# A longer hand-written order for the first phase (60 products and ten weight pieces), and the load of u moved ahead

## The chip, the cores and the metric

One core of a Trainium2 chip runs the whole kernel. The metric is the time of one execution in microseconds (us). The engines are named as in the profile: PE multiplies matrices and transposes, DVE, ACT and POOL work element by element, SP issues the transfers (DMA). Each engine works through its own queue of instructions in order, and waits at an instruction until what it needs has been signalled.

## The reference

```python
# attention: B=2, H=8, S=768, D=48, a state of D x D per head
cur = k_t (outer) v_t, weighted by u
y_t = r_t . (state + cur)
state = w_t * state + k_t (outer) v_t
# x: [1536, 384], the outputs of all heads side by side
# first network: w_in 384 x 2048, w_out 2048 x 384
x = max(0.01 * (x @ w_in), x @ w_in) @ w_out
# second network: a gate over 8 experts, normalised 8 times over rows and columns
P = exp(x @ w_gate - max); 8 times: P /= P.sum(1); P /= P.sum(0); P *= N / E
out = sum over e of P[:, e] * (max(x @ w1[e], 0) @ w2[e])   # 384 -> 1024 -> 384
```

## The kernel before

The program has three phases on PE. The first, here called the front, computes the attention in 12 blocks of 128 tokens (even blocks are one batch, odd ones the other) and starts the first network under it. The second, the middle, finishes the first network and the gate; its first gate product is L579. The third runs the eight experts.

The front's order is written by hand. `FRONT` is a table of single operations, split at the blanks, and the program issues them in that order; each goes to the queue of its engine. Three kinds of names stand in it.

- `7k` is an operation of attention block 7. PE: `w`, `k`, `r` turn the block's inputs (L369), `m` is the scores (L414), `B` turns the keys (L425), `y` the outputs (L446, L455), `z` the new state (L463), `x` turns the result (L496). DVE: `q` and `p` are the two running products of the decays (L387, L392), `K` and `R` weigh keys and r with them (L396), `c` sums r times u times k per head (L510), `A` and `D` mask the scores (L429), `Y` adds to the output (L472), `U` to the state (L487), `l` splits off the low half of the result (L299). POOL: `a`, `b` multiply r, k and u (L504, L505), `v` is L511. ACT has `W`, `S`, `s`, `t`, `C`, `h`. `9Lv` is a load of block 9's v by SP (L349).
- `c6f` is a step of the conversion of weight piece 6. The first network's weights arrive as 64-bit floats; each of 16 pieces (768 KB) is loaded into one of two staging buffers `stg` (L255, SP) and split into a high and a low part. DVE does `a` (L264), `b` (L267), `d` (L270) and `f` (L274), ACT `e`, `g`, `h`, POOL `m` (L278) and `l` (L280). The step `m` is the last reader of the staging buffer, so the load of piece n+2 waits for the `m` of piece n. Pieces come in fours: two of w_in, two of w_out.
- `u5.1P` is a product of the first network: group 5 of a list of column quarters and token groups, half 1. `P` is a first-layer product of 18 matmuls (L531), followed by `r` (ACT), `t` (DVE, L1083), `h` (ACT, L1085), `l` (POOL, L1087). `u5.2p` is a second-layer product of 12 matmuls (L546), followed by `q`, its sum (ACT for the first quarter, DVE L1094 otherwise). One `P` or `p` is one slot; slots go on in the middle.

PE's results in the front lie in six banks that are handed round in turn: an operation that needs a bank takes the one that came free longest ago, and so waits for the operation that frees it.

The middle is not ordered by hand. Its operations are issued slot by slot, `PIECE_AT` names the slot at which the conversion of each piece beyond the table is written, and the framework's scheduler sets the final order on each engine; it may put such an operation between operations of the table. `FRONT_SLOTS` is the number of slots and `FRONT_PIECES` the number of pieces that the table covers; the next two pieces' loads are issued right behind the table.

Of the kernel before, what the change touches and what calls it, by code (L numbers as in the profile page):

```python
# [67 lines left out]


FRONT = """  # L70
0w 0a 0k 0W 0r 0q 0b 1w 0s 0I 0K 0p 0B 0c 0C c0a 0t 0R 1r 1W c0b 0m 0v 1q c0g c0d 1a 1s 1k 0A 0z c0e 0D 1b 1I 1K
0y 0U c0f 1p c0m 1B 2Lw 1C 0Y 2Lk 1t 1z 1c 1R c0h 1v 2Lr c1a c0l 2Lv 0x 1U c1b 1m 0h c2L 2a 0l 2w c1g 1A 2k 2W
2r 1D 2b 2q 1y c1d 2s 2I 2K 3Lw c1e 1Y 2B 3Lk 2p 2S 1x 3Lr 2c 2C 3w 2R 3Lv 1h 2v 2t c1f 2m 3W 1l 3a 3k 3q 2z c1m
3r 2A u0.0P 3s 2D 2U 3b c1h c3L 3I 3K 2y u0.0r 3p c1l u0.0t 3t 3c u0.0h c2a 3B 3S 4Lw 2Y u0.0l u0.1P 3R 4Lk 3C
c2b 3v 4Lr c3a 2x c2g 4Lv 3m c2d u0.1r c3b 2h 4w c2e 4k 4a u0.1t 2l 4W 3z 3A u0.1h 4b 4r 3D c3g 4q 3y u0.1l 3U
4s 4I c2f 4K c2m 4S 5Lw 3Y 4B 4p 5Lk 3x 4C 5Lr c2h 4z 4c 5Lv 3h c2l 4R 4t c4L 3l 4m c3d 5w 4v 4A 5k c3e 5r 4D 5a
u2.0P 5W c3f 5b 5q 4y u2.0r c3m u2.0t 5s 4U 5I 5K c3h c5L u2.1P 5p 5S c3l 4Y 5t 5c 4x 5R 5B 5v 4h c4a u0.0p 5C
6Lw 4l 6Lk c4b 5m u0.0q 6Lr c5a c4g 5z c4d 6Lv 5A c4e 6w 5D 6k 6W u0.1p 5U 6a 6q 5y u0.1q 6b c4f 6s 6I 6K c4m 6r
6p 6S 7Lw 6B u0.2p 7Lk 6C c4h 5Y 7Lr 6z 6c u0.2q c4l u2.0h 6R 7Lv 5x 6t 6U 7w c6L 6m 5h c5b 7W u2.0l 7k 5l c5g
7r 6A u1.0P 6D 6v 7q 7a 6y c5d u1.0r 7b 7s u1.0t c5e 7I 7K 7p u1.0h 7B 7S 8Lw u1.0l u3.0P 6Y 8Lk 7c 7t 7R 7v 8Lr  # L80
u2.1r c5f 7C 6x 8Lv 7m 6h u2.1t c5m 6l 8w u2.1h 8k 7A 8W 7z 7D u2.1l c5h c7L 8q 8r 7y 8a 7U 8s 8I 8K c5l 8p
u2.0p 8S 9Lw 9Lk 8B u2.0q 8b u1.1P 7Y 8C 9Lr 8R 8t 8c 9Lv c7a 8v c6a 7x u1.1r 8m 9a 7h u1.1t 9w 7l u1.1h 9k 8A
9b 9W 8z 8D 9q 9r u1.1l 8y 8U 9s 9I 9K u3.0r 9p 9B 9S 10Lw u2.1p u3.0t 8Y 10Lk 9t 9c 8x 10Lr 9R 9C 9v u2.2p
u2.1q c7b 8h 10Lv 9m 8l c7g c7d 10a c6b u2.2q 10w c7e 10k 9z 10W 10b 9A c6g 10r 9D u3.1P 10q 9U 10s 10I 9y 10K
u3.1r 10p u3.1t 10t 10c u4.0P 10S 11Lw 9Y 10R 10v 11Lk c7f 11Lr 9x u4.0r c6d 10m c7m 9h 11Lv u4.0t c6e 9l 11w
11k 10A u4.0h u4.1P 11a 11W 10D c7h c6f u4.0l 11q 10y 11b 11s 11I 11K c7l 11p 11r 11S u5.0P c6m 10Y 11t 11c 10x
11R u5.1P 10h 11v c6h c8L 10l c6l 11m u5.1r u5.1t u6.0P 11A 11D 11y c8a c8b c8g c8d u1.0p 11Y c8e c8f 11x u1.1p
11h u1.0q c8m 11l u1.2p u1.1q c8h u6.1P u1.2q u3.0h c8l u3.1h u7.0P u3.0l u7.1P u3.1l u4.1r u4.1t u4.1h u5.0r
u3.0p u4.1l u5.0t u3.1p u3.0q u6.0r u6.0t u3.2p u3.1q u4.0p u5.0h u3.2q u5.1h u5.0l u4.1p u4.0q u5.1l u6.1r
u4.2p u4.1q u6.1t u7.0r u5.0p u4.2q u7.0t u6.0h u6.1h u6.0l u5.1p u5.0q u6.1l u7.1r u5.2p u5.1q u7.1t u8.0P  # L90
u5.2q u7.0h u7.1h u7.0l u6.0p u8.0r u7.1l u8.0t u6.1p u6.0q u6.2p u6.1q u7.0p u8.0h u6.2q u8.0l u7.1p u7.0q
u7.2p u7.1q u8.1P u7.2q u9.0P u8.1r u8.1t u8.1h u9.1P u8.1l u9.0r u9.0t u9.0h u8.0p u9.0l u9.1r u9.1t u8.1p
u9.1h u8.0q u9.1l u8.1q
""".split()

FRONT_SLOTS, FRONT_PIECES = 46, 9

GATES = {
    "0/P7": "cs_pe", "0/P14": "cols1", "-1/Q:0:0": "cols2", "0/P0": "rows1", "-1/Q:0:2": "rows2",
# [11 lines left out]
def tile_rwkv__leaky_moe__sinkhorn_moe(  # L111
# [41 lines left out]
    def src(x, i):  # L153
        return x[i % B, :, (i // B) * T : (i // B + 1) * T, :].rearrange("h t d -> t h d")
# [53 lines left out]
    def forward(general, ctx):  # L208
# [43 lines left out]
        def load_words(src):  # L252
            st = stage()
            sv = st.bitcast(I32).rearrange("p (a n t) -> p a n t", a=src.shape[1], t=2)
            nc.sync.dma_start(out=sv.rearrange("p a n t -> p a (n t)"), in_=src)  # L255
            return sv
# [89 lines left out]
        def load_tile(i, names):  # L346
            for n in names:
                t = A.nat[i % 2][n]
                nc.sync.dma_start(out=t[:, :, 0:D], in_=src({"w": w, "k": k, "r": r, "v": v}[n], i))  # L349
# [373 lines left out]
        def piece_load(n):  # L723
            kind, q, h = pieces[n]
            if kind == "i":
                c0 = 2 * (q * FQ + h * NW)
                pst[n] = load_words(w_in32[:, :, c0 : c0 + 2 * NW])
            else:
                pst[n] = load_words(w_out32[:, q * NJ + h * NR : q * NJ + (h + 1) * NR, :])
# [23 lines left out]
        if general:  # L753
            piece_load(0)
        else:
            load_tile(0, "wrk")
            load_tile(1, "w")
            piece_load(0)
            nc.sync.dma_start(
                out=ub.rearrange("p h d -> p (h d)"), in_=u.rearrange("h d -> (h d)").partition_broadcast(P)  # L760
            )
            load_tile(1, "r")
            load_tile(0, "v")
            load_tile(1, "vk")
# [48 lines left out]
        def attach(sl, pe, post, first=False):  # L813
            q = extra.setdefault(sl, [])
            if first:
                q.insert(sum(1 for x in q if x[2]), (pe, post, True))
            else:
                q.append((pe, post, False))

        PIECE_AT = (-7, -4, -1, 0, 0, 1, 1, 5, 44, 56, 57, 60, 81, 85, 85, 90)  # L820

        last = {q: max(n for n, s_ in enumerate(slots) if order[s_[1]][0] == q) for q in range(NQ)}
        lastp1 = {q: max(n for n, s_ in enumerate(slots) if order[s_[1]][0] == q and s_[0] == "p1") for q in range(NQ)}
        for n, (kind, q, h) in enumerate(pieces):
            at = PIECE_AT[n]
            assert at + 1 < need[(kind, q, h)]
# [52 lines left out]
        def w_load(s):  # L879

            st = stage()
            va = st[:, :PW].rearrange("p (c f) -> p c f", c=KD)
            vb = st[:, PW:].rearrange("p (i n) -> p i n", i=2)
            if s < NH:
                e, m = divmod(s, NJ2 // 2)
                nc.sync.dma_start(out=va, in_=w1[e].rearrange("(c p) f -> p c f", p=P)[:, :, m * 2 * P : (m + 1) * 2 * P])
            if s > 0:
                e, m = divmod(s - 1, NJ2 // 2)
                nc.sync.dma_start(
                    out=vb, in_=w2[e].rearrange("(j p) n -> p j n", p=P)[:, 2 * m : 2 * m + 2, :]  # L890
                )
            raw[s] = (va, vb)
# [98 lines left out]
        attach(close_slot, none, open_wb)  # L991
        s4 = PIECE_AT[-1] + 2
        attach(s4, none, lambda: w_load(0))
# [382 lines left out]
    with ExitStack() as es:  # L1376
        forward(False, es)
    flag = nc.values_load(oki)
    with tc.If(flag == 0):
        with ExitStack() as es:  # L1380
            recurrence(es)
        with ExitStack() as es:
            forward(True, es)
# [29 lines left out]
```

## Time and profile before

| | before |
|---|---|
| median of 3 runs (lowest to highest) | 1106.45 us (1106.14 to 1107.18) |
| the profiled execution | 1104.46 us |
| its span in the trace | 1102.7 us |
| PE busy in the span | 1066.0 us (97%) |
| DVE, ACT, POOL busy | 815.4, 485.9, 544.6 us |
| PE's mean granted clock | 0.981 of full |
| the gate's first product (L579) starts at | 308.95 us |

The span is 1.76 us shorter than the execution it was taken from. Some 794 us of the span, from the gate's first product on, hold the gate and the experts, and the change lies ahead of that. A busy PE may still run at half clock, so busy shares are read together with the granted clock.

### The profile page before, as it was taken

How to read it: one execution, taken by the hardware profiler on the slowest of the kernel's cores; microseconds unless marked ns; L12 is line 12 of the kernel's file. 1: busy time of each engine (PE TensorE's matmuls, PEld its weight loads, DVE VectorE, ACT ScalarE, POOL GpSimd, SP SyncE). 2: the span in 40 equal slices, each digit the busy share in tenths (PEclk: the TensorE clock that was granted, in tenths of full speed). 3: DMA queues.
4: the chain of work that ended last, by engine and by line, in shares of the span. 5: the costliest groups of instructions: out<-in, count | busy, mean ns of one | idle time of the engine just before them, and what ended most of it. 6: DMA issues, size and time to landing. Idle time of an engine off the chain costs nothing.

```text
span 1102.7 us, 16354 instructions
## 1 busy us (share of the span) xinstructions
PE 1066.0 (97%) x6295; PEld 980.7 (89%) x6295; DVE 815.4 (74%) x1352; ACT 485.9 (44%) x894; POOL 544.6 (49%) x632
## 2 busy tenths in 40 slices
PE   7899989999999899999999999999999999999997
PEld 6798989999997688899999999999999999999997
DVE  7989954275346998777776777767777777777776
ACT  4546544344334344454444444444444444445431
POOL 6548465258442445464445554455544555445500
PEclk8889989999999999999999999999999999999999
DMA  7446221012000000010000100001000010000002
GB/s 193 94 116 142 69 86 58 1 58 79 23 1 1 29 29 29 29 58 30 29 29 29 58 30 29 29 29 58 30 29 29 29 54 33 29 29 29 15 1 90
DMA packets 79160, 50.90 MB, mean 46 GB/s; under 512 B 51808, under 2 KB 73952, under 8 KB 79072
## 3 DMA queue, kind: packets, MB, share of 16 engines
q1 hardware_dynamic: 79072, 49.76, 15.4%
q8 instruction: 51, 0.84, 0.3%
q14 instruction: 37, 0.30, 0.1%
HBM read 47.39 MB, written 2.36 MB: 45 GB/s over the span
## 4 chain that ended last, share of the span: by engine, by line
PE 81%; DVE 12%; POOL 3%; issue 1%; DMA 1%; ACT 1%; SPq 0%; POOLq 0%; DVEq 0%; ACTq 0%
PE yb L1266 35%; PE m L1223 29%; PE ybm L546 7%; PE hb L531 5%; DVE pf L392 1%; DVE nn L264 1%; DVE nn L267 1%; DVE q L387 1%; PE f L531 1%; PE m L1234 1%; DVE AT L429 1%; DVE t L1083 1%; POOL nn L278 1%; PE f L463 1%; DVE stg L274 1%
## 5 line engine op out<-in xcount | busy, mean ns | idle before, releaser
L1266 PE MATMUL yb<-w,wb 128*128 128x384 f32 x1392 | 277.4, 337 | 3.9 <-DVE small L644 1.5
L1281 DVE SCALAR_TENSOR_TENSOR x2f<-yb,Pm,x2f 128x384 f32<-128x384 f32 x336 | 205.1, 611 | 94.2 <-PE yb L1266 92.6
L1266 PEld LDWEIGHTS yb<-w,wb 128*128 128x128 f32 x1392 | 247.9, 188 | 23.5 <-DVE small L644 1.9
L903 POOL TENSOR_TENSOR w<-stg,w 128x768 fp32r<-128x768 f32 x32 | 59.2, 1851 | 368.1 <-ACT w L901 368.1
L1223 PE MATMUL m<-xr,wc 128*128 128x512 f32 x837 | 231.5, 396 | 0.0
L1295 ACT ACTIVATE sn<-m 128x512 f32<-128x512 f32 x217 | 129.0, 594 | 147.3 <-PE m L1223 147.3
L1266 PE MATMUL yb<-w,hs 128*128 128x384 f32 x912 | 181.5, 337 | 0.6 <-DVE x2f L1281 0.5
L1223 PEld LDWEIGHTS m<-xr,wc 128*128 128x128 f32 x837 | 155.1, 188 | 23.6
L1266 PEld LDWEIGHTS yb<-w,hs 128*128 128x128 f32 x912 | 162.7, 188 | 12.8 <-DVE x2f L1279 1.1
L1303 ACT ACTIVATE wb<-m 128x512 fp32r<-128x512 f32 x79 | 47.0, 597 | 148.4 <-PE m L1223 148.4
L1087 POOL TENSOR_TENSOR gl<-t,gh 128x512 fp32r<-128x512 f32 x48 | 67.3, 1406 | 70.5 <-ACT gh L1085 48.1
L932 POOL TENSOR_TENSOR wc<-wsum,wc 128x768 fp32r<-128x768 f32 (+1 forms) x60 | 101.3, 1709 | 0.0
L950 DVE TENSOR_TENSOR m<-m,sn 128x512 f32<-128x512 f32 x124 | 85.9, 693 | 5.3 <-ACT sn L1295 0.3
L546 PE MATMUL ybm<-gh,wb 128*128 128x256 f32 x576 | 84.0, 289 | 3.0 <-DVE x2f L1094 3.0
L914 POOL TENSOR_TENSOR wsum<-stg 128x128 f32<-128x128 f32 x186 | 83.5, 472 | 0.9 <-DVE wc L932 0.9
L952 DVE TENSOR_TENSOR m<-sn,m 128x512 f32<-128x512 f32 x93 | 64.6, 695 | 24.2 <-PE m L1223 24.1
L1223 PE MATMUL m<-wahi,wc 128*128 128x512 f32 x279 | 80.7, 397 | 0.5 <-DVE m L950 0.5
L1223 PE MATMUL m<-walo,wc 128*128 128x512 f32 x279 | 80.6, 397 | 0.5 <-DVE m L950 0.2
L546 PEld LDWEIGHTS ybm<-gh,wb 128*128 128x128 f32 x576 | 75.9, 195 | 4.8 <-DVE x2f L1094 3.3
L1303 ACT ACTIVATE hs<-m 128x512 fp32r<-128x512 f32 x51 | 30.5, 598 | 107.0 <-PE m L1223 107.0
L1305 DVE SCALAR_TENSOR_TENSOR wb<-m,wb 128x512 fp32r<-128x512 f32 x79 | 54.3, 687 | 10.6 <-ACT wb L1303 8.7
L1223 PEld LDWEIGHTS m<-wahi,wc 128*128 128x128 f32 x279 | 51.2, 188 | 7.5 <-DVE m L950 0.8
(179 smaller groups left out, 1706.6 us busy)
## 6 DMA issues: line engine op xcount, KB each, us to landing
stg<-in_moe_w_dram SPq DMA_DIRECT2D x64, 384.0 KB, 3.6
stg<-in_moe_w_in_dram SPq DMA_DIRECT2D x8, 768.0 KB, 4.7
stg<-in_moe_w_out_dram SPq DMA_DIRECT2D x8, 768.0 KB, 4.4
wn<-in_w_dram SPq DMA_DIRECT2D x12, 192.0 KB, 4.5
rn<-in_r_dram SPq DMA_DIRECT2D x12, 192.0 KB, 5.0
kn<-in_k_dram SPq DMA_DIRECT2D x12, 192.0 KB, 4.4
vn<-in_v_dram SPq DMA_DIRECT2D x12, 192.0 KB, 3.0
out_dram<-x2f SPq DMA_DIRECT2D x12, 192.0 KB, 1.9
```

The costliest lines, as they stand in the source:

```text
L531: nc.tensor.matmul(hb[:, s * GC : (s + 1) * GC], wt[:, c, f0 : f0 + P], x_part(xt, c, g * GC, GC), start=(n == 0), stop=(n == 3 * KD - 1),)
L546: nc.tensor.matmul(yb[:, :GC], wt[:, j, d * P : (d + 1) * P], gt[:, j, :], start=(n == 0), stop=(n == 3 * NJ - 1),)
L914: nc.gpsimd.tensor_tensor(sums[:, n, :], get(x), get(y), op=ALU.add if sg > 0 else ALU.subtract)
L932: eng.tensor_tensor(l, src, h.bitcast(F32), op=ALU.subtract)
L950: eng.tensor_tensor(out, x, y, op=ALU.add if sy > 0 else ALU.subtract)
L952: eng.tensor_tensor(out, y, x, op=ALU.subtract)
L1087: nc.gpsimd.tensor_tensor(gl[:, 2 * j : 2 * j + 2, :], tv, gv.bitcast(F32), op=ALU.subtract)
L1223: nc.tensor.matmul(b, wt, xt, start=start and k == 0, stop=k == 2, skip_group_check=True)
L1266: nc.tensor.matmul(yb[:, :DM], hv[:, hk, i, t * P : (t + 1) * P], wv[:, wk, i, :], start=n == 0, stop=n == 5)
L1281: nc.vector.scalar_tensor_tensor(out=av, in0=yb, scalar=Pm[:, i, e : e + 1], in1=av, op0=ALU.mult, op1=ALU.add)
L1295: nc.scalar.activation(t, psum(S, f[1]), AF.Copy)
L1303: nc.scalar.activation(h, v, AF.Relu)
```

## The change

The table is written anew: the same attention operations in another order, six more first-layer products and eight more second-layer ones, so that it covers 60 slots and the ten pieces 0 to 9, where it covered 46 slots and the nine pieces 0 to 8. `PIECE_AT` moves pieces 10 and 11 behind the table's end. The load of `u` is issued ahead of the second block's decays and of piece 0. No operation is added to the program or taken away, and from the gate's first product on PE's order is as it was.

```diff
-11R u5.1P 10h 11v c6h c8L 10l c6l 11m u5.1r u5.1t u6.0P 11A 11D 11y c8a c8b c8g c8d u1.0p 11Y c8e c8f 11x u1.1p
...
+u4.1h 9q u3.1p 10Lv u4.1l c8h 8x u3.0q u5.0P 9S u3.1q 9I 9K 9v 9p u6.0r 8h c8l 9s u3.2p u6.0t u5.0r 8l 9t u5.0t
+10a u4.0p u3.2q u5.0h 9R 10b u4.1p c9d u4.0q u5.0l 10c u4.2p c9e u4.1q c9f 9m u4.2q u6.0h c9m u5.1P 9A 9D u6.0l
+c9h 9B u5.1r 9y 9C c9l u5.1t u5.1h u5.1l 9z 9Y 9x 9U 11Lw 10v 10w 9h 10k 10W 11Lk 9l 10r 10q u5.0p 11Lr 11Lv 10S
...
-FRONT_SLOTS, FRONT_PIECES = 46, 9
+FRONT_SLOTS, FRONT_PIECES = 60, 10
...
             load_tile(0, "wrk")
-            load_tile(1, "w")
-            piece_load(0)
             nc.sync.dma_start(
                 out=ub.rearrange("p h d -> p (h d)"), in_=u.rearrange("h d -> (h d)").partition_broadcast(P)
             )
+            load_tile(1, "w")
+            piece_load(0)
             load_tile(1, "r")
...
-        PIECE_AT = (-7, -4, -1, 0, 0, 1, 1, 5, 44, 56, 57, 60, 81, 85, 85, 90)
+        PIECE_AT = (-7, -4, -1, 0, 0, 1, 1, 5, 44, 56, 60, 61, 81, 85, 85, 90)
```

In the rows below the lines of the changed kernel are three higher in the code ahead of the loads (L264 becomes L267). The first place is SP's queue at the very beginning; `wn`, `kn`, `rn`, `vn` are the inputs, with 112 to 115 for the second block, and `spare` is where `u` is put. Before:

```order
L349 DMA kn_109<-in_k_dram 128x8x48
L349 DMA wn_112<-in_w_dram 128x8x48
L255 DMA stg<-in_moe_w_in_dram 128x3x512
L759 DMA spare<-in_u_dram 128x384
L349 DMA rn_114<-in_r_dram 128x8x48
```

In the changed kernel:

```order
L352 DMA kn_109<-in_k_dram 128x8x48
L760 DMA spare<-in_u_dram 128x384
L352 DMA wn_112<-in_w_dram 128x8x48
L258 DMA stg<-in_moe_w_in_dram 128x3x512
L352 DMA rn_114<-in_r_dram 128x8x48
```

In the changed kernel the load of `u` has gone ahead of two loads, and these stand one place later.

The second place is DVE's queue where the scheduler has put conversions that are not in the table between the last blocks' operations. Before, at block 11 (`11R`, the low half `10l`, then the masks `11A`, `11D`), with `stg_1895` for piece 9 and `stg_1380` for piece 8:

```order
L396 TENSOR_TENSOR R_122<-f0_182,pf_118 128x512
L299 TENSOR_TENSOR xr2_91<-f2_184,xr2_91 128x3x128
L264 TENSOR_SCALAR nn1_107<-stg_1895 128x768
L267 SCALAR_TENSOR_TENSOR nn1_107<-stg_1895,nn1_107 128x768
L1083 SCALAR_TENSOR_TENSOR t1_2_105<-f3_185,t1_2_105 128x512
L270 TENSOR_SCALAR stg_1895<-stg_1895 128x768
L429 TENSOR_TENSOR AT0_123<-f1_183,spare_80 128x512
L429 TENSOR_TENSOR AT1_124<-f0_182,spare_80 128x512
```

In the changed kernel, at block 9 (from `c9f` over the masks `9A`, `9D` and `u5.1t` to `9Y`), with `stg_1176` for piece 9, `stg_2150` for piece 10 and `stg_2152` for piece 11:

```order
L277 SCALAR_TENSOR_TENSOR stg_1176<-stg_1176 128x768
L273 TENSOR_SCALAR stg_2150<-stg_2150 128x768
L432 TENSOR_TENSOR AT0_123<-f1_183,spare_80 128x512
L432 TENSOR_TENSOR AT1_124<-f0_182,spare_80 128x512
L277 SCALAR_TENSOR_TENSOR stg_2150<-stg_2150 128x768
L1086 SCALAR_TENSOR_TENSOR t1_2_105<-f3_185,t1_2_105 128x512
L267 TENSOR_SCALAR nn1_107<-stg_2152 128x768
L270 SCALAR_TENSOR_TENSOR nn1_107<-stg_2152,nn1_107 128x768
L475 TENSOR_TENSOR y_129<-f4_186,cv_127 128x384
```

Piece 9 is no longer such a piece; pieces 10 and 11 are, and they stand two blocks earlier, among the operations of block 9.

The third place is SP's queue at the same point of the program, behind the loads of block 11. Before (`stg_1380` and `stg_1895` are pieces 8 and 9, the two behind them 10 and 11):

```order
L349 DMA rn1_114<-in_r_dram 128x8x48
L349 DMA vn1_115<-in_v_dram 128x8x48
L255 DMA stg_1380<-in_moe_w_in_dram 128x3x512
L255 DMA stg_1895<-in_moe_w_in_dram 128x3x512
L255 DMA stg_1897<-in_moe_w_out_dram 128x2x768
L255 DMA stg_2133<-in_moe_w_out_dram 128x2x768
```

In the changed kernel (`stg_2150` and `stg_2152` are pieces 10 and 11, `stg_2205` is piece 12):

```order
L352 DMA rn1_114<-in_r_dram 128x8x48
L258 DMA stg_2150<-in_moe_w_out_dram 128x2x768
L258 DMA stg_2152<-in_moe_w_out_dram 128x2x768
L258 DMA stg_2205<-in_moe_w_in_dram 128x3x512
L352 DMA vn1_115<-in_v_dram 128x8x48
```

Two pieces fewer are loaded behind the last block, and three loads of pieces now stand ahead of block 11's v.

## Rows read from the trace of the kernel before

**Rows 1.** Windows of core 0: window, us, busy us (and instructions), granted clock, DMA

```profile
45.60:65.20 19.60, 16.17 (x81) 15.11 (x81) 15.92 (x22) 9.59 (x19) 9.93 (x9) 0.56 0.30 73
87.10:146.00 58.90, 57.19 (x522) 54.62 (x521) 53.94 (x76) 34.15 (x77) 40.60 (x28) 1.00 0.42 98
146.00:160.80 14.80, 10.38 (x48) 10.12 (x49) 10.57 (x14) 5.11 (x6) 5.68 (x3) 0.65 0.21 74
160.80:204.20 43.40, 42.40 (x350) 41.86 (x349) 18.76 (x29) 19.67 (x36) 22.99 (x17) 1.00 0.18 55
```

**Rows 2.** Chain of waits, the opening: start us, us, what

```profile
2.55 1.28 SPq L349
...
4.62 5.22 DMA spare<-in_u_dram
...
9.97 1.01 POOL rk L505
...
12.77 2.08 PE f L414 x16
```

**Rows 3.** Timeline of DVE: start us, us, line, operation, [idle before <-releaser]

```profile
37.94 2.87 DVE L392 TENSOR_TENSOR_SCAN pf<-wS,rP 128x516 f32<-128x516 f32 x1
...
57.02 0.56 DVE L472 TENSOR_TENSOR y<-f,cv 128x384 f32<-128x384 f32 x1 [2.52 <-PE f L455]
...
62.60 1.29 DVE L429 TENSOR_TENSOR AT<-f,spare 128x512 f32<-128x512 f32 x2 [1.08 <-PE f L414]
...
68.19 0.69 DVE L1083 SCALAR_TENSOR_TENSOR t<-f,t 128x512 f32<-128x512 f32 x1 [1.97 <-ACT t L1081]
...
133.82 1.35 DVE L274 SCALAR_TENSOR_TENSOR stg<-stg 128x768 int32<-128x768 int32 x1
...
138.10 1.22 DVE L392 TENSOR_TENSOR_SCAN pf<-wS,rP 128x516 f32<-128x516 f32 x1
...
140.15 0.68 DVE L396 TENSOR_TENSOR R<-f,pf 128x512 f32<-128x512 f32 x1
...
147.61 0.56 DVE L264 TENSOR_SCALAR nn<-stg 128x768 int32<-128x768 int32 x1 [6.12 <-DMA stg<-in_moe_w_in_dram]
```

**Rows 4.** Timeline of PE, same columns

```profile
49.05 2.02 PE L463 MATMUL f<-vn,Kb 128*128 128x96 f32 x8 [3.43 <-DVE t L1083]
...
121.74 1.03 PE L463 MATMUL f<-vn,Kb 128*128 128x96 f32 x8
...
125.19 0.36 PE L446 MATMUL f<-Sp,R 128*128 128x96 f32 x2
...
127.40 0.57 PE L455 MATMUL f<-vn,AT 128*128 128x48 f32 x4
...
130.46 1.16 PE L414 MATMUL f<-R,K 48*128 48x128 f32 x16
...
149.82 0.46 PE L446 MATMUL f<-Sp,R 128*128 128x96 f32 x2 [3.85 <-DVE t L1083]
150.89 1.25 PE L455 MATMUL f<-vn,AT 128*128 128x48 f32 x4 [0.60 <-DVE AT L429]
```

**Rows 5.** Chain of waits from 138 to 148 us

```profile
140.96 1.84 POOL nn L278
...
142.83 4.69 DMA stg<-in_moe_w_in_dram
```

**Rows 6.** Chain of waits at full PE: a first-layer product

```profile
204.15 2.16 PE hb L531 x18
```

**Rows 7.** DVE's groups by shape, 0 to 330 us: count | busy us, mean ns

```profile
L267 DVE SCALAR_TENSOR_TENSOR nn<-stg,nn 128x768 int32<-128x768 int32 x16 | 20.7, 1300 | 0.1
...
L264 DVE TENSOR_SCALAR nn<-stg 128x768 int32<-128x768 int32 x16 | 17.1, 1080 | 7.7 <-DMA stg<-in_moe_w_in_dram 6.1 <-POOL walo L280 0.8 <-POOL win3lo L280 0.8
L274 DVE SCALAR_TENSOR_TENSOR stg<-stg 128x768 int32<-128x768 int32 x16 | 17.0, 1066 | 0.9 <-ACT stg L273 0.9
...
L270 DVE TENSOR_SCALAR stg<-stg 128x768 int32<-128x768 int32 x16 | 14.5, 913 | 0.1
```

More of the change, by code (lines that the diff above doesn't have):

```diff
@@ L70 @@
 FRONT = """
[L71 to L85, printed above, removed]
@@ L86 @@
-11k 10A u4.0h u4.1P 11a 11W 10D c7h c6f u4.0l 11q 10y 11b 11s 11I 11K c7l 11p 11r 11S u5.0P c6m 10Y 11t 11c 10x
-11R u5.1P 10h 11v c6h c8L 10l c6l 11m u5.1r u5.1t u6.0P 11A 11D 11y c8a c8b c8g c8d u1.0p 11Y c8e c8f 11x u1.1p
-11h u1.0q c8m 11l u1.2p u1.1q c8h u6.1P u1.2q u3.0h c8l u3.1h u7.0P u3.0l u7.1P u3.1l u4.1r u4.1t u4.1h u5.0r
-u3.0p u4.1l u5.0t u3.1p u3.0q u6.0r u6.0t u3.2p u3.1q u4.0p u5.0h u3.2q u5.1h u5.0l u4.1p u4.0q u5.1l u6.1r
-u4.2p u4.1q u6.1t u7.0r u5.0p u4.2q u7.0t u6.0h u6.1h u6.0l u5.1p u5.0q u6.1l u7.1r u5.2p u5.1q u7.1t u8.0P
@@ L91 @@
-u5.2q u7.0h u7.1h u7.0l u6.0p u8.0r u7.1l u8.0t u6.1p u6.0q u6.2p u6.1q u7.0p u8.0h u6.2q u8.0l u7.1p u7.0q
-u7.2p u7.1q u8.1P u7.2q u9.0P u8.1r u8.1t u8.1h u9.1P u8.1l u9.0r u9.0t u9.0h u8.0p u9.0l u9.1r u9.1t u8.1p
-u9.1h u8.0q u9.1l u8.1q
+0w 0a 0k 0W 0r 0q 0b 1w 0s 0I 0K 0p 0B 0c 0C 0R 0t c0a 0m 1W c0b 1q c0g 0v 0z 0A 1s 0D 1a 1k c0d 0U 0y 1b 1I 1K
+c0e 1p c0f 1t 1r 1c 2Lw c0m 0Y 1B 1R 2Lk 0x c1a 1C 2Lr 1m 1v c0h c1b 2Lv 0h c0l c2L 0l c1g 1z c1d 2a 1A c1e 2w
+1D 2b 1U 2k c1f 2W 1y 2q c1m 2c 2s 2r 2I 2K 3Lw 2S 1Y 2B 3Lk 2p 1x 2v c1h 3Lr 1h c2a c1l 2C 3w 2R 3Lv 2t 2z 1l
@@ new lines @@
+c3L c2b 3W 2m 3a 2U c2g u0.0P 2A 3b 2D 3q 2y u0.0r 3c 3s u0.0t 3I c2d u0.0h 3p c2e u0.0l 3k 4Lw 3r 3S 2Y u0.1P
+4Lk 3K 3v 3t 3R 4Lr c2f 4Lv 2x u0.1r c3a 3m c2m 2h u0.1t 2l 3B u0.1h 4w 3A 3C 4k u0.1l 3D c4L c2h 3z c3b 4W 3y
+c2l 3U c3g 4q 4a 4r 5Lw 3Y 4S 4I 4K 3x 4b 5Lk 4p 3h 4B 4s 5Lr 4C 5w 3l 5Lv 4t 4z 4c 4R 5W 4v 5k c3d 4m 5a 4U c3e
+5r 4A u2.0P 5b 4D c3f 5q 4y c3m u2.0r u2.0t 5s 5I 5K c3h c5L 5p 5B 5S u2.1P c3l 4Y 5c 5C 5R 5t c4a 5v u0.0p c4b
+6Lw u0.1p 6Lk c4g c4d c5a 6Lr u0.0q c4e c5b u0.2p 6Lv u0.1q c4f c5g 4x 5m c5d u0.2q c4m u2.0h 4h 5z 5A c5e 4l 6w
@@ new lines @@
+u2.0l c4h c6L 5D 6k 6r 5U 6W 5y c5f c4l 6q 6a u1.0P 7Lw 5Y 6S 6I 6K c5m 7Lk 6p 6s 7Lr 5x u1.0r 6B 5h 7Lv u3.0P
+6b 6C u1.0t 6t c7L 5l 6R u1.0h 6c c5h 6m u1.0l c6a 6z 6v u2.1r 6A 7w u2.1t 7a 7k 7W 6D 7r u2.1h u4.0P 6U c5l 7q
+6y u2.1l c6b 7s 7b u4.0r 7I 7K c6g u4.0t u1.1P 8Lw 7S 6Y 7p 8Lk 8Lr 7c 7t u2.0p 7R 7v u1.1r 8Lv c6d u2.1p u2.0q
+u1.1t c6e 8a c7a u2.2p u1.1h u2.1q u1.1l c6f 6x u2.2q u3.1P u4.0h 8b c7b u3.0r 6h u4.0l u3.0t c7g 7m 6l u3.1r
+c6m c7d 7B 8w 7C 8k 8W 7z u3.1t c6h c8L 8r 7A c7e u4.1P c6l 7D 7U 8q 7y c7f 8s 8I 8K c7m 8p 8B 8S 9Lw u6.0P 9Lk
@@ new lines @@
+8C 7Y c7h 9Lr 8c 8t 8R 7x c7l 9Lv 8z c8a 7h c9L 8m 8v 7l u1.0p 8A 9a 8D u1.1p 8U 9b u1.0q c8b u1.2p u1.1q c8g 9c
+8y u1.2q u3.0h c9a u3.1h c8d u3.0l c9b c8e u3.1l u4.1r 9w c8f 10Lw c9g 9k 9r 10Lk 9W u3.0p u4.1t c8m 10Lr 8Y
+u4.1h 9q u3.1p 10Lv u4.1l c8h 8x u3.0q u5.0P 9S u3.1q 9I 9K 9v 9p u6.0r 8h c8l 9s u3.2p u6.0t u5.0r 8l 9t u5.0t
+10a u4.0p u3.2q u5.0h 9R 10b u4.1p c9d u4.0q u5.0l 10c u4.2p c9e u4.1q c9f 9m u4.2q u6.0h c9m u5.1P 9A 9D u6.0l
+c9h 9B u5.1r 9y 9C c9l u5.1t u5.1h u5.1l 9z 9Y 9x 9U 11Lw 10v 10w 9h 10k 10W 11Lk 9l 10r 10q u5.0p 11Lr 11Lv 10S
@@ new lines @@
+10I 10K u5.1p 10p u5.0q 10s u5.2p 11a 10R u5.1q 10t 11b 10m u5.2q u6.1P 11c 10A 10D 10y u6.1r u6.1t u6.1h u6.1l
+11w 10Y 11k 11W 10x 11v 11r 11q 10h u6.0p 10l 11S u6.1p 11I u6.0q 11K 11s 11p u6.2p u6.1q 11t 11R u7.0P u6.2q
+11m u7.0r u7.0t u7.1P 11A u7.0h 11D u7.0l 11y u7.1r u7.1t u7.1h u7.1l u8.0P 11Y 11x u8.0r u7.0p 11h u8.0t 11l
+u8.0h u7.1p u7.0q u8.0l u7.2p u7.1q u8.1P u7.2q u9.0P u8.1r u8.1t u8.1h u9.1P u8.1l u9.0r u9.0t u9.0h u8.0p
+u9.0l u9.1r u9.1t u8.1p u9.1h u8.0q u9.1l u8.2p u8.1q u9.0p u8.2q u9.1p u9.0q u9.2p u9.1q u10.0P u9.2q u10.1P
@@ L94 @@
+u10.0r u10.0t u10.0h u11.0P u10.0l u10.1r u10.1t u10.1h u11.1P u10.1l u11.0r u11.0t u11.0h u10.0p u11.0l u11.1r
+u11.1t u10.1p u11.1h u10.0q u11.1l u10.2p u10.1q u11.0p u10.2q u12.0P u11.0q u12.1P u12.0r u12.0t u12.0h u12.0l
+u12.1r u12.1t u12.1h u12.1l
 """.split()
-FRONT_SLOTS, FRONT_PIECES = 46, 9
+FRONT_SLOTS, FRONT_PIECES = 60, 10
 GATES = {
```

## The prediction

> **What bounds the kernel now.** I read the windows first. From the gate on, PE's order is the same in both kernels, so everything is decided in the first 309 us. There the windows show two kinds of stage [rows 1]. From 87 to 146 us DVE is busy 53.94 us of 58.90 and PE 57.19: both are nearly full, and up to there it is DVE that paces, because it carries the attention and the conversions of pieces 0 to 7 while PE fills its time with products. From 160.8 to 204.2 us DVE is busy 18.76 us of 43.40 and PE 42.40: PE paces, and time is PE's work. Between and before lie two stages in which PE ran at a low clock, 0.56 from 45.6 to 65.2 us and 0.65 from 146 to 160.8 us.
>
> Then I read what went before these stages. In PE's timeline a new state (L463) waits 3.43 us at 45.6 us and an output (L446) 3.85 us at 146 us, the next output 0.60 us more; both long waits end with DVE's L1083 [rows 4], the operation that hands a bank back. DVE's timeline shows why [rows 3]. At 147.61 us L264 had stood 6.12 us waiting for a load, and `u5.1t` was queued behind it. By DVE's order this L264 is not `c8a` of the table: it is piece 9, put there by the scheduler. Its load waits for `c6m` on POOL. `c6f` ended on DVE at 135.17 us (133.82 and 1.35), `c6m` began at 140.96 us, so POOL lost 5.8 us to what stood ahead of it, and the load took 4.69 us more [rows 5].
>
> The clock is the second half of each stall. A clock of 0.65 over 14.80 us is 10.4 us at half speed (1.2 instead of 2.4 GHz), a loss of 5.2 us where PE paces. A clock of 0.56 over 19.60 us is 17.2 us at half speed; there DVE paced, and the loss is what DVE then waited for PE: 2.52, 1.08 and 1.97 us, together 5.6 us [rows 1, 3].
>
> **The change, part by part.** *The load of u.* In the chain of the opening it is issued at 4.62 us, lands 5.22 us later, and POOL's L505, DVE and then the first scores at 12.77 us follow without a gap [rows 2]. It now goes out where the second block's decays went, at 2.55 us: **-2.0**. Bounds 0 (the second block's decays, 0.5 us later, or the half clock of the opening takes it) and -2.1.
>
> *The stage from 45.6 us.* Before, four conversion steps (`c2b`, `c3a`, `c2d`, `c3b`) stood on DVE directly ahead of `u0.1t`: 1.30 + 1.08 + 0.91 + 1.30 = 4.6 us [rows 7]. Now `c2f` and `c3a` stand there, 2.1 us. 2.5 us less leaves 0.9 us of the 3.43 us wait, nearest to the 0.60 us one [rows 4], and I take it that the clock holds: **-5.6**, bounds -5.6 and 0.
>
> *Up to block 6.* Ahead of `6R` DVE now also has `5l`, `c5b`, `c5d`, `c5f`, `u1.0t` and no longer `6U`: 1.30 + 0.91 + 1.07 from the groups [rows 7] and some 0.6 net for the small ones, +3.8 us. PE by then has also done two first-layer products and not `6z` and `7w`: 2 x 2.16 [rows 6] less 1.03 [rows 4] less 0.4 is 2.9 us that need not be done later. Net **+0.9**, bounds 0 and +3.8.
>
> *From block 6 on.* A second-layer product has 12 matmuls where a first-layer one has 18 in 2.16 us [rows 6], so 1.44 us. Ahead of `11x` stand four more `P` and fourteen more `p`, 4 x 2.16 + 14 x 1.44 = 28.8 us of PE's work that DVE's attention can hide behind. I therefore take PE as the pacer from block 6 on, and its idle times of before count as won: 58.90 - 57.19 = **-1.7**, and 43.40 - 42.40 = **-1.0** [rows 1]. Bounds 0 and their whole for each.
>
> *The stage from 146 us.* Piece 9 is now in the table, its load waits for `c7m`, and between `c7f` and `c9a` stand some 17 DVE operations or 11 us, against 1.84 + 4.69 = 6.5 us for `c7m` and a load [rows 5]. So that stall goes: 14.80 - 10.38 = 4.4 idle and 5.2 of half clock, **-9.6**, bounds -9.6 and 0.
>
> *What stands in its place.* The scheduler now puts pieces 10 and 11 between the table's operations, and the load of piece 11 waits for `c9m`, which needs `c9f`. Take the end of `u3.2p` on PE as zero. DVE then has `u3.2q`, `9R`, `c9d`, `c10a`, `10c`, `c10b`, `c9f`: 0.68 [rows 3] + 0.91 + 1.08 + 1.30 + 1.07 [rows 7] and about 1.0 for the two small ones, 6.0 us. `c9m` 1.84 and the load 4.69 [rows 5] bring 12.6 us. `c11a` 1.08 and `c11b` 1.30 [rows 7] stand ahead of `9Y`, 0.56 [rows 3]: 15.5 us. PE meanwhile has three `p` (4.3), `9m` 1.16, `u5.1P` 2.16, `9B` 0.4, `9y` 2.8 (125.19 to 127.97), `9z` 1.03 [rows 4, 6] and then `9x`, which needs `9Y`: 11.9 us. PE waits 3.6 us. Behind `9Y` DVE has `c11d`, `9U`, `c11f`, `9l`, `10q`, `10K`, `10p`, `10R`, some 7.2 us, and PE up to `10m` 6.1 us: 1.1 us more. Together **+4.7**. With both L264 at 0.56 us [rows 3] the wait at `9x` is 2.6 us. Bounds 0 (rival C) and 10.5, if `c9m` waits in POOL's queue as `c6m` did, 5.8 us. A wait of 3.6 us lies beside those of 3.43 and 3.85 us, after which the clock was low. Here second-layer products follow directly, where before the outputs of block 11 came first, so I take two thirds of the 5.2 us: **+3.5**, bounds 0 and 8.6 (half of 17.2).
>
> *Small waits.* Through blocks 8 and 9 DVE and PE have nearly equal work, some 12 us each from `8R` to `8x` by the same rows, so some of PE's cover is thin: **+1.5**, bounds 0 and +4. Pieces 12 to 15 are converted at the slots where they were; I count nothing for them.
>
> One row speaks against packing conversions closer: the product of decays L392 took 2.87 us at 37.94 us and 1.22 us at 138.10 us [rows 3], with POOL at work beside the former. The change puts two more POOL operations ahead of `6m`; if each held DVE up for 1.65 us, the difference of the two rows, the sum would be 3.3 us higher.
> The Trainium skill, SBUF — State Buffer, section "SBUF: two separate sides", says that a DVE operation with two SBUF inputs and a GpSimd operation that reads SBUF take one port pair as an exclusive lock, and the later one is blocked for the whole of the other.
> By that rule the sum would be 3.3 us higher; the two rows agree in kind, and no row shows who held the port.
>
> The sum is -2.0 - 5.6 + 0.9 - 1.7 - 1.0 - 9.6 + 4.7 + 3.5 + 1.5 = -9.3 us. It is made against the profiled execution of 1104.46 us (span 1102.7 us and 1.76 us around it), giving 1095.2 us. The median of the runs was 2.0 us above the profiled one, so I predict 1097.2 us.
>
> **Rivals.** *A, as summed:* 1097.2 us, by itself 1092 to 1101 us.
> *B, the stage from 45.6 us stays:* if PE there waits 2 us or more, for instance because the longer table puts other conversions ahead of a bank's release, the clock is low as before and 5.6 us come back: 1102.8 us. For it: DVE paces there in both kernels, and 2.5 us less work ahead of one release is all that I can point to.
> *C, no new stall:* if PE lags DVE by 4 us more at `u3.2p` than I count, `9Y` is ready when PE comes: 8.2 us less, 1089.0 us. For it: from 87 to 146 us PE idled 1.7 us in all [rows 1]. Against it: `u3.2q` waits for `u3.2p` itself, so DVE cannot run ahead there.
> *D, the other side:* `c9m` is held up on POOL by 5.8 us as `c6m` was; piece 11's load then lands 5.8 us later, PE's idle time is 4.7 + 5.8 = 10.5 us and half clock costs 8.6 us, in all 10.9 us above A: 1108.1 us. The old time is reached where `c9m` is held up 4.2 us, 0.2% above it at 6.4 us. Against it: `u5.0l`, which stands ahead of `c9m`, has its input early.
> *E, nothing:* the table moves stalls about and gives back what it wins, 1105 to 1107 us.
> *F, POOL beside DVE:* the two POOL operations ahead of `6m` cost the 3.3 us priced above, 1100.5 us. This is what the Trainium skill's page SBUF — State Buffer would give here.
>
> **How the numbers follow.** A 0.45, B 0.17, C 0.14, D 0.12, E 0.07, F 0.05. The forecast is A's. What a measurement here can tell from no change is about 0.2%, 2.2 us, so faster means below 1104.2 us. Faster: A 0.44, B 0.12, C 0.14, D 0.01, E 0.03, F 0.04, in all 0.78. Within 0.2%: A 0.01, B 0.04, D 0.04, E 0.02, in all 0.11. Slower: B 0.01, D 0.07, E 0.02, F 0.01, in all 0.11. The range takes in C at 1089 and B with some of E: 1088 to 1105 us.
>
> **What would show it.** The first scores start at about 10.7 us. No window of 15 us between 40 and 80 us has a clock under 0.8. L264 of piece 11 shows a wait for its load of some 3 us at block 9, and L496 behind it a wait for L472 of about 3.6 us, with a lower clock after it. No other wait on PE between blocks 7 and 11 is over 1.5 us. L579 starts at about 299.6 us. The prediction is wrong if a half-clock stage of over 10 us remains, if waits for other loads stand on DVE, or if the middle, from `11x` to L579, has PE idle for over 5 us because the conversions of pieces 12 to 15 are now late.

## The result, and the profile after

The changed kernel took 1095.12 us (median of 5 runs, 1094.70 to 1097.25), the kernel before 1106.14 us on the same chip (5 runs, 1102.47 to 1107.18): a ratio of 0.9907, interval 0.9891 to 0.9923, or 10.3 us less (the medians alone differ by 11.0). Forecast were 1097.2 us. The profiled run of 1094.70 us has a span of 1093.0 us and a mean granted clock of 0.990 (before 0.981), and the gate's first product (now L582) starts at 298.56 us, 10.4 us earlier; forecast were 299.6 us. Behind the gate 0.7 us is given back: the span is 9.7 us shorter. Lines are three higher than in the rows of before (L463 is L466, L264 is L267, L1083 is L1086).

Windows of core 0 of the changed kernel, columns as in [rows 1]:

```profile
22.30:37.10 14.80, 13.71 (x71) 12.31 (x71) 14.59 (x17) 8.03 (x18) 10.70 (x8) 0.54 0.69 180
37.10:84.60 47.50, 44.97 (x402) 42.33 (x401) 46.11 (x67) 30.09 (x66) 34.55 (x23) 1.00 0.51 119
84.60:144.90 60.30, 58.65 (x519) 57.05 (x519) 57.16 (x75) 36.80 (x72) 46.61 (x30) 1.00 0.43 106
...
150.10:158.90 8.80, 8.80 (x51) 8.70 (x51) 8.18 (x11) 5.55 (x14) 6.38 (x4) 0.66 0.35 97
158.90:223.00 64.10, 63.93 (x549) 63.32 (x548) 26.13 (x41) 24.06 (x46) 19.98 (x15) 1.00 0.03 10
223.00:241.00 18.00, 16.23 (x133) 16.03 (x134) 17.93 (x23) 7.88 (x11) 9.93 (x5) 1.00 0.28 88
...
84.61:298.56 213.95, 205.22 (x1731) 202.63 (x1732) 137.50 (x191) 98.77 (x183) 124.15 (x96) 0.98 0.22 60
```

Read the clock column first. The two low stages of [rows 1], 0.56 over 19.60 us and 0.65 over 14.80 us, are gone from their places in the program. In their stead there is one in the opening, 0.54 from 22.3 to 37.1 us, where the DMA engines are busy for 0.69 of the time, and one of 0.66 from 150.1 to 158.9 us: nearly the time of the old one, but in block 9, where that was in block 11. Before the second one PE waited, as its timeline shows:

```profile
10.96 1.97 PE L417 MATMUL f<-R,K 48*128 48x128 f32 x16
...
21.58 0.55 PE L499 MATMUL f<-ident,y 128*128 128x128 f32 x3 [3.21 <-DVE y L475]
...
54.07 0.55 PE L499 MATMUL f<-ident,y 128*128 128x128 f32 x3 [0.83 <-DVE y L475]
...
84.61 1.16 PE L417 MATMUL f<-R,K 48*128 48x128 f32 x16 [0.42 <-DVE R L399]
...
150.10 0.90 PE L499 MATMUL f<-ident,y 128*128 128x128 f32 x3 [5.16 <-DVE y L475]
...
298.56 0.63 PE L582 MATMUL lgb<-xr,wgp 128*16 128x512 f32 x2
```

The wait of 5.16 us at 150.10 us is `9x`, the place that the prediction named, and the releaser is `9Y` on DVE. In [rows 4] it had been 3.85 us two blocks later. DVE's timeline shows what stood ahead of `9Y`:

```profile
137.07 1.58 DVE L270 SCALAR_TENSOR_TENSOR nn<-stg,nn 128x768 int32<-128x768 int32 x1
...
146.06 1.57 DVE L267 TENSOR_SCALAR nn<-stg 128x768 int32<-128x768 int32 x1 [2.25 <-DMA stg<-in_moe_w_out_dram]
147.67 1.90 DVE L270 SCALAR_TENSOR_TENSOR nn<-stg,nn 128x768 int32<-128x768 int32 x1
149.50 0.55 DVE L475 TENSOR_TENSOR y<-f,cv 128x384 f32<-128x384 f32 x1
...
237.57 0.96 DVE L270 SCALAR_TENSOR_TENSOR nn<-stg,nn 128x768 int32<-128x768 int32 x1
```

L267 and L270 at 146 and 148 us are piece 11, put there by the scheduler; `9Y` (L475) is through its 0.55 us at once when they are done. The chain of waits says why they were late:

```profile
139.59 2.14 POOL nn L281
...
141.75 4.22 DMA stg<-in_moe_w_out_dram
...
146.06 1.59 DVE nn L267
...
147.67 1.90 DVE nn L270
...
149.57 0.48 DVE y L475
...
150.10 0.90 PE f L499 x3
```

It is the pattern of [rows 5]: `c9m` on POOL, the load that waited for it, then the conversion. Only `c9m` began here as soon as its input was there, where `c6m` had been held up for 5.8 us.

### The profile page after: what moved, and what is told of

The parts are those of the page before. It is cut to its first block, busy times and chain, and to the rows that moved or that the text cites. A ratio compares the mean times of both kernels' runs of the same rounds, so it can differ in the third digit from the quotient of the medians.

```text
span 1093.0 us, 16362 instructions
## 1 busy us (share of the span) xinstructions
PE 1056.0 (97%) x6295; PEld 971.2 (89%) x6295; DVE 820.3 (75%) x1352; ACT 486.3 (44%) x894; POOL 546.3 (50%) x632
## 4 chain that ended last, share of the span: by engine, by line
PE 81%; DVE 12%; POOL 2%; issue 2%; ACT 1%; DMA 1%; SPq 0%; POOLq 0%; DVEq 0%; ACTq 0%
PE yb L1269 36%; PE m L1226 29%; PE ybm L549 7%; PE hb L534 3%; PE f L534 3%; DVE nn L270 2%; DVE q L390 1%; DVE nn L267 1%; DVE stg L277 1%; DVE t L1086 1%; PE m L1237 1%; DVE stg L273 1%; DVE AT L432 1%; DMA stg<-in_moe_w_in_dram 1%; DVE pf L395 1%
```

## Experiments

Each ratio is against the kernel before on the same chip. E1, E3 and E5 edit the kernel before, the others the changed one.

**E1, the load of u alone, and E2, everything but that load.**

```diff
+            nc.sync.dma_start(out=ub..., in_=u...)
             load_tile(1, "w")
             piece_load(0)
-            nc.sync.dma_start(out=ub..., in_=u...)
```

> The kernel before with nothing but the load of u moved ahead of the second block's decays and of piece 0. If the chain of the opening sets the end (my term of -2.0 us), the first scores start at about 10.9 instead of 12.77 us and the program ends 1 to 2 us earlier. Rival: DVE paces behind the opening and the 1.8 us are given back there, as in the changed kernel, whose block 0 was turned (L499) only 0.3 us earlier than before: then the time is within 0.5 us of before.

> The changed kernel with only the load of u put back behind the second block's decays and piece 0. If u's lead is worth its 2.0 us in the new order, it is 1.5 to 2 us slower than the changed kernel, about 1097 us. Rival: block 0's sum (L475) waits on DVE behind four other operations whatever u does, then it is within 0.5 us of the changed kernel.

E1 took 1107.05 us (12 runs), ratio 1.0012 [1.0002, 1.0022]; E2, with the edit taken back in the changed kernel, 1093.63 us, 0.9896 [0.9878, 0.9914]. The load's move wins nothing: E1 is 0.2 to 2.4 us slower than the kernel before, and E2 is not told apart from the changed kernel. In E1 the chain of the opening and then PE's timeline show what took its place:

```profile
4.81 6.75 DMA rn<-in_r_dram
```

```profile
11.70 1.09 PE L369 MATMUL f<-ident,rn 128*128 128x128 f32 x4 [0.71 <-DMA rn<-in_r_dram]
...
17.38 3.54 PE L455 MATMUL f<-vn,AT 128*128 128x48 f32 x16
```

u lands early, but block 1's r takes 6.75 us to land (before 5.39), the transposes of block 1 stand ahead of the first scores in PE's queue, and the scores start at 12.71 us (before 12.77). Behind them the 16 matmuls of L455 take 3.54 us, before 1.93. In the changed kernel they do start at 10.96 us, and by `0x` 0.3 us of that is left: 21.58 us against 21.92.

**E3, the kernel before with piece 9 written into its table,** behind `11x`; the scheduler had put it between block 11's operations.

```diff
-11R u5.1P 10h 11v c6h c8L 10l c6l 11m ...
-11h u1.0q c8m 11l u1.2p u1.1q c8h u6.1P u1.2q u3.0h c8l u3.1h u7.0P ...
+11R u5.1P 10h 11v c6h c8L 10l c6l c9L 11m ...
+11h u1.0q c8m 11l c9a u1.2p u1.1q c9b c8h u6.1P c9g c9d u1.2q c9e u3.0h c9f c8l u3.1h c9m c9h c9l u7.0P ...
...
-FRONT_SLOTS, FRONT_PIECES = 46, 9
+FRONT_SLOTS, FRONT_PIECES = 46, 10
```

> The kernel before with piece 9 taken into its table: its load directly behind piece 8's, its steps behind 11x, nothing else moved; the products of the table stay 46. If the stall from 146 us is the scheduler's piece 9 standing ahead of u5.1t with a late load, the wait of 3.85 us and the low clock from 150 us go, and the program ends 8 to 10 us earlier, near 1096 us. Rival: the gain came from the 14 additional products under the attention; then this is worth under 2 us.

1109.51 us (8 runs), 1.0035 [1.0021, 1.0049]: slower. Its windows:

```profile
146.00:160.80 14.80, 14.80 (x128) 14.80 (x127) 12.92 (x17) 6.15 (x8) 6.39 (x4) 1.00 0.26 93
160.80:180.00 19.20, 9.66 (x51) 8.87 (x50) 13.26 (x13) 7.89 (x12) 13.68 (x9) 0.64 0.35 100
```

and PE's timeline in the second:

```profile
167.77 0.80 PE L546 MATMUL ybm<-gl,wb 128*128 128x256 f32 x2 [6.11 <-POOL gl L1087]
```

The first window is the stage of 146 us of [rows 1], now full and at full clock: the cause of that stall was piece 9's place. But now pieces 10 and 11 are the ones outside the table, the scheduler puts them ahead of the second-layer work, and PE is idle 9.5 us of the next 19.2 at a clock of 0.64. Taking a piece into the table moves the stall to the next piece. The rival of E3, that the gain of the change lies in the 14 products more under the attention, is not ruled out by this: no run moves the products alone.

**E4, the changed kernel with pieces 10 and 11 written late into the table,** so that the scheduler has none left to put forward.

```diff
-... 11Lr 11Lv 10S
+... 11Lr 11Lv c10L c11L 10S
...
+c10a c10b u8.0h u7.1p c10g c10d u7.0q u8.0l c10e u7.2p u7.1q c11a u8.1P u7.2q c10f c11b u9.0P u8.1r u8.1t c10m ...
...
-FRONT_SLOTS, FRONT_PIECES = 60, 10
+FRONT_SLOTS, FRONT_PIECES = 60, 12
```

> The changed kernel with pieces 10 and 11 taken into its table too, their steps behind 11l, so that the scheduler can no longer put them between the operations of block 9. If the wait of 5.16 us at 9x and the low clock after it come from piece 11's late load, both go, and the program ends 7 to 9 us earlier, near 1087 us. Rival: PE runs out of work at block 9 because DVE has the attention's work as well as products' sums to do, and the wait only moves to another place: within 3 us of the changed kernel.

1094.91 us, 0.9905 [0.9887, 0.9923], the same as the changed kernel. Yet the wait at `9x` is gone. The window from `9m` to `10m`, which in the changed kernel is 21.50 us long (137.44 to 158.94, the next `L417`), is here

```profile
139.64:153.01 13.37, 13.37 (x122) 13.12 (x121) 8.98 (x14) 7.33 (x18) 9.85 (x8) 1.00 0.35 100
```

without a gap and at full clock: 8.1 us less, the whole price of the stall. But 5.2 of these 8.1 us came back later, a part of them here, in PE's timeline:

```profile
180.83 1.63 PE L549 MATMUL ybm<-gh,wb 128*128 128x256 f32 x8 [2.08 <-DVE x2f L1097]
```

There a second-layer sum stands on DVE behind `c10a`, `c10b` and `c10d`. A lower clock follows, 0.68 up to 186.20 us, a loss of 1.7 us beside the wait of 2.1. From the scores of block 6 to the gate E4 takes 211.03 us (213.95 in the changed kernel), and its opening was 2.2 us longer, though its table is the same up to there.

**E5, the kernel before with the bank of the stage from 45.6 us handed back sooner,** by which `u0.1r` stands ahead of `c3a` and `u0.1t` ahead of `c2d` and `c3b`.

```diff
-c2b 3v 4Lr c3a 2x c2g 4Lv 3m c2d u0.1r c3b 2h 4w c2e 4k 4a u0.1t 2l ...
+c2b 3v 4Lr u0.1r c3a 2x c2g 4Lv 3m u0.1t c2d c3b 2h 4w c2e 4k 4a 2l ...
```

> The kernel before with one token moved twice: u0.1r ahead of c3a, and u0.1t, which hands back the bank that a new state waits for, ahead of c2d and c3b. If the low clock from 48 to 65 us follows from the wait of 3.43 us behind these conversions, the wait falls under 1 us, the clock stays full there, and the program ends 4 to 6 us earlier, near 1100 us. Rival: the small matmuls of that stage hold the clock low whatever waited before them, or DVE, which paces there, takes the same time anyway: within 1.5 us of before.

1103.43 us (12 runs), 0.9985 [0.9972, 0.9998]: 1.6 us by the ratio (0.2 to 3.1), not 4 to 6. The wait of 3.43 us [rows 4] is gone, but

```profile
45.00:65.00 20.00, 17.91 (x120) 16.30 (x117) 17.23 (x23) 10.27 (x21) 13.38 (x10) 0.74 0.34 80
```

0.74 over 20 us is still 10.4 us at half clock, where [rows 1] had 17.2. PE's longest wait there is now 1.70 us, at 49.32 us, for DVE.

**E7, the changed kernel with the first block's sum `0Y` ahead of `c0f` and `1c`.**

```diff
-c0e 1p c0f 1t 1r 1c 2Lw c0m 0Y 1B ...
+c0e 1p 0Y c0f 1t 1r 1c 2Lw c0m 1B ...
```

> The changed kernel with block 0's sum (0Y, L475) moved on DVE ahead of c0f and 1c. If the wait of 3.21 us at 0x and the low clock from 22.5 to 37 us are what took back u's 1.8 us, the wait falls under 1 us and the program ends 1 to 3 us earlier. Rival: DVE paces from block 0 to block 4, so that PE's wait there costs nothing: within 0.7 us.

1095.51 us, 0.9912 [0.9898, 0.9927]: nothing. PE's timeline:

```profile
19.77 0.55 PE L499 MATMUL f<-ident,y 128*128 128x128 f32 x3 [0.76 <-DVE y L475]
```

The wait of 3.21 us fell to 0.76 us, and waits of 1.47 and 1.12 us came behind it: in the opening DVE paces, and its order only moves PE's waits.

**E8 and E10, two other places for pieces 10 and 11; E9 and E11, the same with the edits of E7 and E2 besides.** E8 spreads the steps over the products of groups 9 to 12. E10 writes piece 10 where the scheduler had put it, and starts piece 11 only behind `10R`:

```diff
-... 10a u4.0p u3.2q u5.0h 9R 10b u4.1p c9d u4.0q u5.0l 10c u4.2p c9e u4.1q c9f 9m u4.2q u6.0h c9m u5.1P 9A 9D u6.0l
+... 10a u4.0p u3.2q u5.0h 9R 10b u4.1p c9d c10a u4.0q u5.0l 10c c10b u4.2p c9e u4.1q c9f c10g c10d 9m u4.2q u6.0h c10e c9m c11L u5.1P 9A 9D u6.0l
...
+... 10m u5.2q u6.1P 11c c11a 10A 10D 10y u6.1r c11b u6.1t u6.1h c11g u6.1l
+11w c11d 10Y 11k 11W c11e 10x ...
+11m u7.0r c11f u7.0t c11m u7.1P ...
```

> As the run with pieces 10 and 11 late, but their steps stand further back, one or two between the products of groups 9 to 12, where DVE has no sums of the first quarter to do. If that run lost 5 of the 8 us it had won at block 9 to conversions standing ahead of a sum that PE waited for (2.08 us at 180.8 us, and the low clock after it), these stay won: no wait of over 1.4 us from 11x to the gate and about 1089 us. Rival: the work of the two conversions cannot be hidden behind block 11 at all, and the time stays within 2 us of the changed kernel.

> The run with pieces 10 and 11 spread, and with it block 0's sum ahead of c0f and 1c and the load of u back behind piece 0. If the opening's terms add to the others, 1 to 3 us earlier than that run alone; if the opening is paced by DVE and its loads whatever their order, the same within 1 us.

> The changed kernel with piece 10 in the table at the places where the scheduler had put it, and piece 11 in it from 10R to 11m, where DVE waits 1.2 to 2.3 us at a time for PE. The two runs before won 8.1 us from 9m to 10m and lost 4 to 5 of them behind 11x, where sums on DVE and ACT stood behind conversion steps. If that is so, this keeps the 8 us: no wait at 9x, none over 1.4 us behind 11x, 1087 to 1089 us. Rival: conversions anywhere in blocks 10 and 11 make DVE late for PE again, 1091 us or more.

> The same with block 0's sum ahead of c0f and 1c and the load of u back behind piece 0, as in the run with everything. If these two are worth the 1.7 us by which that run's median was ahead of the one without them, 1085 to 1087 us; if they are within the spread of the opening, the same as the run without them within 1 us.

| | median, us | ratio to before, interval | block 6's scores to the gate, us |
|---|---|---|---|
| changed kernel | 1095.12 | 0.9907 [0.9891, 0.9923] | 213.95 |
| E8 | 1092.75 | 0.9877 [0.9863, 0.9892] | 209.81 |
| E9 | 1091.08 | 0.9869 [0.9851, 0.9886] | 208.71 |
| E10 | 1091.47 | 0.9870 [0.9853, 0.9886] | 207.75 |
| E11 | 1090.14 | 0.9856 [0.9833, 0.9879] | 207.98 |

E10's window from the scores of block 6 to the gate, and its one new wait on PE:

```profile
88.53:296.28 207.75, 202.51 (x1731) 199.89 (x1731) 135.03 (x191) 98.68 (x183) 123.94 (x96) 1.00 0.22 62
```

```profile
153.37 0.50 PE L549 MATMUL ybm<-gl,wb 128*128 128x256 f32 x2 [1.71 <-POOL gl L1090]
```

The same 1731 matmuls as in the changed kernel, in 6.2 us less, all at full clock. E10 was expected at 1087 to 1089 us and took 1091.47: its opening was 3.9 us longer than the changed kernel's, though the table is the same up to there. E11 has the lowest median of the study; its interval, like those of E9 and E10, lies below the changed kernel's, and the three are not told apart. E8 in its place waits 1.02 and 1.34 us for second-layer sums on ACT.

## Why the prediction was right, and where its terms were not

The time, the direction and the case (A) came as forecast: 1095.12 us beside 1097.2. Two errors of opposite sign lie in the sum of -9.3 us, which shows when it is cut at the scores of block 6: of the gain, 1.3 us too much was forecast ahead of them and 2.4 us too little behind. That the sum came so near the 9.7 us by which the span fell is in part luck.

**Up to block 6.** Forecast were -2.0 - 5.6 + 3.8 = -3.8 us there, measured is 87.13 to 84.61 us, -2.5.
- The load of u, -2.0, fell. The step that failed is that everything behind it in the opening's chain would move with it. E1 and E2 agree that it wins nothing: the loads of the opening push one another, and what DVE has to do up to `0x` takes the rest.
- The stage from 45.6 us, -5.6, was the right mechanism at too large a size. "I take it that the clock holds" was right of that stage (1.00 from 37.1 to 84.6 us), but 0.54 over 14.8 us stands ahead of it, 13.6 us at half clock. So one of the prediction's own signs of being wrong, a half-clock stage of over 10 us, did come, in a place that it had not named. E5, which hands back that one bank sooner and does nothing else, wins 1.6 us, but keeps 10.4 us at half clock. Where DVE paces, PE's half clock costs only what DVE waits for PE, and that was over-counted.
- The +3.8 is said to stand ahead of `6R`, but `6U` stood behind `6R` in the old table too; the sum holds for what stands ahead of `6m`.

How the 2.5 us divide among the terms, and whether they are the change's at all, cannot be read from one trace. The scores of block 6 came at 84.61, 86.77, 87.59 and 88.53 us in the changed kernel, E4, E8 and E10, whose tables are the same up to there, and at 87.13 and 88.09 us in the kernel before and E3, which share the old one. Why equal tables differ can be seen: in the first four, DVE, ACT, POOL and SP work through the same instructions in the same order, and up to 38 us DVE is only 0.55 us later in E4 than in the changed kernel. Then, in windows of the changed kernel and of E4, and in E4's DVE timeline:

```profile
37.00:45.60 8.60, 8.60 (x82) 8.38 (x82) 8.55 (x15) 5.39 (x12) 5.60 (x5) 1.00 0.29 59
...
37.00:45.60 8.60, 8.60 (x65) 8.21 (x65) 7.05 (x12) 3.51 (x6) 3.98 (x4) 0.74 0.12 24
...
39.75 1.29 DVE L432 TENSOR_TENSOR AT<-f,spare 128x512 f32<-128x512 f32 x2 [0.65 <-PE f L417]
...
43.51 0.69 DVE L1086 SCALAR_TENSOR_TENSOR t<-f,t 128x512 f32<-128x512 f32 x1 [0.89 <-ACT t L1084]
```

In this stretch PE has the first network's first products, and half clock in it makes DVE wait 0.65 and 0.89 us; in the changed kernel, whose half clock lay ahead of it, DVE waits nowhere from 37 to 66 us. E10 has the same two waits (0.65 and 1.04 us) and a third of 1.41 us at 63.22 us, in a stretch (58 to 64 us) at 0.72. So the openings differ for the most part by the place at which the half clock fell.

**From block 6 to the gate.** Forecast were the other terms less the 2.9 us of products done earlier: -1.7 - 1.0 - 9.6 + 4.7 + 3.5 + 1.5 - 2.9 = -5.5 us. Measured is 221.82 to 213.95 us, -7.9; the window of before is the second of the two shown below.
- The stage from 146 us, -9.6: its cause is shown by E3. By itself the cure is worth less than nothing there (1.0035), as the next pieces stand in the same way; the sum had that as a term of its own.
- The new wait, +4.7, and its half clock, +3.5: measured 5.16 us at `9x`, none at `10m`, and 0.66 over 8.80 us, 6.0 us at half clock or a loss of 3.0. Together 8.2 us where 8.2 were forecast, with two errors of 0.5 us that cancel, and E4, which takes the stall away, shows 8.1 us. Inside the term, the load was waited for 2.25 us instead of some 3, and `c11a` and `c11b` took 1.57 + 1.90 us instead of 1.08 + 1.30.
- PE as the pacer, -1.7 - 1.0, less the small waits, +1.5: PE idled 1.65 us of 60.30 and 0.17 of 64.10, where before it was 1.71 and 1.00 us [rows 1], so -0.9 beside -1.2. The second part was won, the first not.
- "I count nothing" for pieces 12 to 15 was wrong by about 2 us, in the change's favour. Before, the first of these two windows held that conversion:

```profile
244.00:254.00 10.00, 7.96 (x52) 7.58 (x51) 9.57 (x14) 4.11 (x6) 4.25 (x3) 0.83 0.09 30
...
87.13:308.95 221.82, 212.64 (x1755) 208.84 (x1755) 136.68 (x195) 101.18 (x188) 128.59 (x99) 0.97 0.22 62
```

It is 2.0 us idle and 1.7 us lost at half clock; in the changed kernel PE idles 1.8 us from 223 to 241 us and keeps its clock. About 0.7 us of the -7.9 stay unassigned.

**The rivals.** B fell: no low clock from 37.1 to 84.6 us. C fell: the stall came, and E10 is what C would have been, less the opening. D fell: `c9m` began 0.1 us after `c9f`, as POOL had been free for 1.76 us. E fell by the result. F's 3.3 us did not come, but its mechanism is in the rows. POOL's timeline in the changed kernel:

```profile
136.22 1.60 POOL L1090 TENSOR_TENSOR gl<-t,gh 128x512 fp32r<-128x512 f32 x1
...
147.18 1.58 POOL L1090 TENSOR_TENSOR gl<-t,gh 128x512 fp32r<-128x512 f32 x1
```

L270 starts at 137.07 and at 147.67 us while one of these runs, takes 1.58 and 1.90 us, and ends some 0.8 us behind it; at 237.57 us, with POOL idle, it takes 0.96 us. So it is with all 32 of these steps up to 330 us in the two kernels: the 20 that start while a POOL operation runs end 0.81 to 0.82 us behind that operation, the other 12 take 0.94 to 0.96 us. L267 at 146.06 us, with one input, takes 1.57 us instead of 0.56 [rows 3]. Up to the scores of block 6 the two steps and the product of decays (L392) took 6.8 us more than they do without POOL in the kernel before and 5.3 us in the changed one, so nothing was added there.
The Trainium skill, SBUF — State Buffer, section "SBUF: two separate sides", has a DVE operation with two SBUF inputs and a GpSimd operation that reads SBUF exclude each other on a shared port pair; the trace agrees with it in these 20 steps, and no run here shows the port itself.

**Open.** What moves the half clock in equal openings, by which they differ by up to 3.9 us; and whether u's early load costs something. E1 is slower than the kernel before, and E2, E9 and E11, which have the load back, are 1.2 to 1.7 us ahead of the kernels without that edit, but each of these three intervals overlaps with the other kernel's, and E9 and E11 carry E7's edit too.

## What to carry to other kernels

Where a scheduler may put operations ahead of a hand-written order, look at what it takes from behind the table's end: a conversion whose load is not back stalls an in-order queue, and lengthening the table moves that stall to the next piece; written out at places where the load has landed (E10), pieces 10 and 11 cost 6.2 us less from block 6 to the gate (the medians differ by 3.7 us, as E10's opening was longer). Price a stall on the pacing engine as its wait and the half clock behind it together (here 5.2 + 3.0 us). Where another engine paces, a wait taken away comes back a little later, and a load moved ahead in a full queue only makes its neighbours late.

## What the runs showed that was not expected

- A load of 192 KB moved ahead by two places made the r of block 1 land 6.75 us after its issue instead of 5.39, and nothing was won (E1).
- Waits of PE were followed by low clock at lengths that differ widely: 5.16 us by 8.8 us at 0.66, 3.21 us by 14.8 us at 0.54, 6.11 us in E3 by 0.64 over the window it lies in, 2.08 us in E4 by 0.68, and 1.70 us in E5 by 0.74 over the window it lies in. The waits of 0.83 us at 54.07 us and of 1.71 us in E10 stand in stages at 1.00. No length of the wait alone tells these cases apart.
- A conversion step of 128x768 on DVE takes 0.96 us, or up to 1.90 us in the stall, by the rest of the POOL operation that is running when it starts. `c11a` and `c11b` took 1.1 us more together than the forecast had for them.
